# Seven tiny row loads on ScalarE's transfer queue in the second to last pair of heads, and another order of VectorE's last stage, in a decode step of gated attention with its gradients

## The chip, the core and the metric

The kernel runs on one core of one Trainium2 chip. The time is device microseconds of one execution; lower is better. A core has TensorE (PE), VectorE (DVE), ScalarE (ACT), GpSimd (POOL) and SyncE (SP), each with its own queue of instructions that it takes in order, and 16 transfer (DMA) engines that move data between HBM and the on-chip memory. SP, ACT and POOL start transfers.

## The reference

One token (D = 640) goes through attention over a cache of 4096 keys and values in 32 heads of 128, beside a small dense block with a mish activation (1728 wide); a gate g mixes the two. The kernel computes the output and the gradients of nine of the ten inputs:

```
q = (x @ wq) per head;  s = q . K * 128**-0.5;  p = softmax(s)
a = (p @ V, all heads) @ wo
h = x @ w1 + b1;  b = (h * tanh(softplus(h))) @ w2
g = sigmoid(sum(x * gate_w));  out = g * a + (1 - g) * b
gradients of sum(out * grad_out) for x, K, V, wq, wo, w1, b1, w2, gate_w
```

K and V are 33.6 MB each in bfloat16, and dK and dV as large, so nearly all of the 164 MB moved are the cache read once and its gradient written once. Since a head has one query, dV is the outer product of p and the gradient of the head's output, and dK that of the score's gradient and q.

## The kernel before

The heads are worked in 16 pairs (i = 0 to 15), four pairs to a group g. K and V of a pair are one tile each of 128 partitions x 64 keys x 128 (2 MB); seven such buffers are reused in turn. A buffer's K or V is overwritten in place by dK or dV, stored, and loaded anew by `pump` when its store has landed.

A pair is 16 slots (`slot`, from L743). In slots 0 to 7 PE transposes V in eighths into PSUM, ACT copies each to a `tch` tile (L377), and two slots later PE multiplies it with the output's gradient (L384, dP); in slots 8 to 15 the same is done with the next pair's K (S). The softmax of the pair runs in slots 2 to 8, the sums over V and K (o, dq, L433) in slots 7, 8, 13 and 14. DVE makes dV in four quarters of 128 x 2048 in slots 9, 10, 12 and 13 and dK in slot 15 and slots 0, 1 and 3 of the pair after (`outer`, L465, 1.2 us each). PSUM holds three transposed eighths. Other work is hung into slots by `plan` and `at`: `side` has a list of functions for each (pair, slot), which run in order at the slot's end. DVE sums wq against dq (`dx_sum`, L486), ACT then scales it into dwq in place (`dwq_row`, L352), and dwq is stored in column pieces: the first half by ACT in slot 8 of pair 12, the rest by POOL. The schedule is by hand: each engine's queue has its instructions in the order in which the program names them.

The last pair (i = 15) runs slots 0 to 7 and then a tail written out by hand: `last_dv(t)` and `last_dk(t)` make quarter t and, after quarters 1 and 3, start a store of half the tile on SP (L875, L881). Between them stand the o row, the last a columns, eight dwo rows on ACT with two stores of dwo on ACT (L358), five dx sums on DVE and five dwq rows on ACT. Last come the gate's gradient (L918 to L935), five transposes of the final rows (L939), their copy by DVE (L941) and three small stores on POOL (L944).

A transfer signals its landing on a semaphore. In the built program the transfers that SP and ACT start take eight semaphores in turn (numbers 0 to 7 below), nearly in the order in which the program names them, whichever of the two starts them; POOL's take eight of their own. A start is preceded by a wait for the last user of its semaphore, unless the engine has waited for that before. Around the change, in that order:

```
semaphore  start                          
0          SP   load V of pair 13
1          SP   load K of pair 14
2          SP   load V of pair 14
3          ACT  store dwq, columns of groups 0 and 1 (2560 KB)
4          SP   load K of pair 15
5          SP   load V of pair 15
6          SP   store dK of pair 12
7          SP   store dV of pair 13
0          SP   store dK of pair 13
1          SP   store dV of pair 14
```

Of the kernel before, what the change touches and what calls it, by code (L numbers as in the profile page):

```python
# [12 lines left out]
BF16 = mybir.dt.bfloat16  # L13
# [4 lines left out]
def kernel(  # L18
# [33 lines left out]
    nc = tc.nc  # L52
# [49 lines left out]
    def C(shape, dt, name):  # L102
        return const.tile(shape, dt, name=name, tag=name)
# [116 lines left out]
    def misc(shape, dt, name):  # L220
        return one_ps.tile(shape, dt, name=name, tag="misc")

    def chain(shape, dt, name):
        return one_ps.tile(shape, dt, name=name, tag="chain")
# [99 lines left out]
    def o_rows(g):  # L324
        ps = misc([P, 16, 8], F32, "o8_ps")
        nc.tensor.matmul(ps[:].rearrange("p a b -> p (a b)"), lhsT=od16[:].rearrange("p a b -> p (a b)"), rhs=idb[:],
                         start=True, stop=True)
        o8m = two.tile([P, 16, 8], F32, name="o8m", tag="o8m", bufs=1)
        nc.vector.tensor_tensor(o8m[:], ps[:], m16[:].unsqueeze(2).to_broadcast([P, 16, 8]), ALU.mult)
        nc.vector.reduce_sum(o8f[:], o8m[:].rearrange("p a b -> p b a"), axis=AX.X)  # L330
        nc.vector.tensor_copy(o8[:], o8f[:])

    def a_cols(g, c0=0, c1=RC):
        if c0 == 0:
            mst["a"] = misc([P, RC + W], F32, "a_ps")
        ps = mst["a"][:, 0:RC]
        wv = wob[g % 2][:].rearrange("p k (n c) -> p k c n", c=RC)
        for c in range(c0, c1):
            for k in range(8):
                nc.tensor.matmul(mst["a"][:, c:c + W], lhsT=wv[:, k, c, :], rhs=o8[:, k:k + 1].to_broadcast([P, W]),  # L340
                                 start=(k == 0), stop=(k == 7))
        if c1 == RC:
            if g == 0:
                nc.vector.tensor_copy(a_acc[:], ps)
            else:
                nc.vector.tensor_tensor(a_acc[:], a_acc[:], ps, ALU.add)

    def scaled(eng, dst, src, col):
        if eng is nc.vector:
            nc.vector.tensor_scalar(dst, src, col, None, ALU.mult)  # L350
        else:
            nc.scalar.mul(dst, src, col)  # L352
# [4 lines left out]
    def st_dwo(g, eng, k0=0, k1=8):  # L357
        eng.dma_start(dwo_v[g][:, k0:k1], wob[g % 2][:, k0:k1])  # L358
# [103 lines left out]
    def outer(b, col, row, q):  # L462
        n = J // 4
        j0 = q * n
        nc.vector.tensor_tensor(  # L465
            kview(b)[:, j0:j0 + n, :].rearrange("p j (a b) -> p j a b", b=2),
            col[:, j0:j0 + n, :].unsqueeze(2).to_broadcast([P, n, Dh // 2, 2]),
            row.rearrange("p (a b) -> p a b", b=2).unsqueeze(1).to_broadcast([P, n, Dh // 2, 2]),
            ALU.mult)
# [5 lines left out]
    def dq_row(i):  # L475
        dqb = two.tile([P, 2], BF16, name="dqb", tag="dqb")
        nc.vector.tensor_copy(dqb[:], st[i]["dq"][:, 0:2])  # L477
        ps = chain([P, 2, P], BF16, "dqr_ps")
        for hh in range(2):
            nc.tensor.transpose(ps[:, hh, :], dqb[:, hh:hh + 1].to_broadcast([P, P]), idb[:])  # L480
        c = 256 * (i % 4)
        nc.scalar.copy(dqrow[(i // 4) % 2][:, c:c + 256].rearrange("p (a b) -> p a b", a=2), ps[:])
# [6 lines left out]
    def dwq_row(g, c0, c1, rc, eng=nc.scalar):  # L489
        scaled(eng, wqa[:, rc, g * GC + c0:g * GC + c1], dqrow[g % 2][:, c0:c1], xf[:, rc:rc + 1])  # L490

    def st_dwq(c0, c1, eng):
        eng.dma_start(dwq_v[:, :, c0:c1], wqa[:, :, c0:c1])
# [126 lines left out]
    def at(i, s, f, *a):  # L620
        side.setdefault((i, s), []).append(lambda: f(*a))

    def plan(i, table):
        for s, tasks in table.items():
            for t in tasks:
                at(i, s, *t)
# [76 lines left out]
    plan(12, {8: [(st_dwq, 0, HC, nc.scalar)]})  # L703
    plan(14, {6: [(st_dwq, HC, HC + GC, nc.gpsimd)]})

    CA, CB = GC // 2, 3 * GC // 4
    g, i = NG - 1, NP - 2
    for k, s in enumerate((5, 6, 7, 14, 15)):
# [162 lines left out]
    def last_dv(t):  # L871
        outer(vbuf[i], st[i]["p"], Dr[g % 2][:, q, :], t)
        if t % 2:
            h = slice((t - 1) * KVW // 4, (t + 1) * KVW // 4)
            nc.sync.dma_start(dVv[i][:, h], bufs[vbuf[i]][:, h])  # L875

    def last_dk(t):
        outer(fb, st[i]["ds"], Qr[g % 2][:, q, :], t)
        if t % 2:
            h = slice((t - 1) * KVW // 4, (t + 1) * KVW // 4)  # L880
            nc.sync.dma_start(dKv[i][:, h], bufs[fb][:, h])  # L881
# [12 lines left out]
    last_dv(0)  # L894
    for rc in range(RC):
        dwq_row(g, CA, CB, rc)
    o_rows(g)
    dq_row(i)
    last_dv(1)
    a_cols(g)  # L900
    for k in range(8):
        dwo_row(g, k)
        if k % 4 == 3:
            st_dwo(g, nc.scalar, k - 3, k + 1)
    last_dv(2)
    last_dv(3)
    last_dk(0)
    last_dk(1)
    for rc in range(RC):
        dx_sum(g, NG + g, CB, GC, rc)  # L910
        dwq_row(g, CB, GC, rc)
    st_dwq(g * GC + CA, (g + 1) * GC, nc.gpsimd)
    last_dk(2)
    last_dk(3)

    fin = C([P, 3, RC], BF16, "fin")
    ga = C([P, RC], F32, "ga")
# [8 lines left out]
                                   accum_out=dgp[:])  # L926
    dg_ps = chain([P, 1], F32, "dg_ps")
    nc.tensor.matmul(dg_ps[:], lhsT=ones_f[:], rhs=dgp[:], start=True, stop=True)
    dz = C([P, 1], F32, "dz")
    nc.vector.tensor_scalar(dz[:], dg_ps[:], g_all[:], omg[:], ALU.mult, ALU.mult)  # L930
    nc.vector.tensor_scalar(fin[:, 2, :], xf[:], dz[:], None, ALU.mult)
# [5 lines left out]
    fr_ps = misc([3, RC, P], BF16, "fr_ps")  # L937
    for c in range(RC):
        nc.tensor.transpose(fr_ps[:, c, :], fin[:, :, c], idb[:])  # L939
    frow = C([3, P, RC], BF16, "frow")  # L940
    nc.vector.tensor_copy(frow[:].rearrange("r p c -> r c p"), fr_ps[:])  # L941
    for r, v in enumerate((out_0.rearrange("a b n -> (a b) n"), out_1.rearrange("a b n -> (a b) n"),
# [31 lines left out]
```

## Time and profile before

| | |
|---|---|
| median of 2 runs | 406.71 us (406.62 to 406.8) |
| the profiled execution | 405.83 us |
| its span, first to last instruction | 404.0 us |
| busy: PE, DVE, ACT, POOL | 297.2, 285.6, 246.8, 25.2 us |
| moved | 164.88 MB, mean 408 GB/s |
| mean granted clock of PE | 0.901 |

Times below count from the start of the span. In the profile's lists a line has the start, the length, the engine, the source line and operation, what is written and read, and the count; in brackets is the idle time before it and what ended it. "SPq" and "ACTq" are starts of transfers. A line of a stretch has its bounds and length, the busy time of PE, PE's weight loads, DVE, ACT and POOL with their counts, PE's granted clock, the share of time that the 16 transfer engines were busy, and GB/s.

### The profile page before, as it was taken

Reading aid. Unit: us, or ns where it says so; the run is one execution under the profiler, and the core shown is the slowest. Engines: PE = TensorE matmul, PEld = TensorE weight load, DVE = VectorE, ACT = ScalarE, POOL = GpSimd, SP = SyncE. Lnnn points to the kernel's source line nnn. Section 1 sums busy time; section 2 is a strip of 40 time slices with the busy share of each in tenths; the row PEclk is TensorE's granted clock in tenths of the full one; section 3 lists DMA queues with packets and bytes.
Section 4 is the critical chain, followed back from the end, with each engine's and each line's share of the span. In section 5 each row is a group of like instructions: output and inputs, shape, how many; then the busy total and the mean of one; then the engine's idle time right before and its main releaser. Section 6 shows DMA issues by size and latency. Waiting matters only on the chain.

```text
span 404.0 us, 13041 instructions
## 1 busy us (share of the span) xinstructions
PE 297.2 (74%) x5654; PEld 272.9 (68%) x5657; DVE 285.6 (71%) x618; ACT 246.8 (61%) x507; POOL 25.2 (6%) x50
## 2 busy tenths in 40 slices
PE   4878996998885888673989869732989897987110
PEld 3558986877775777673889769732789786886100
DVE  2767695699975969583797839642695988597930
ACT  3555462586668678761766567731567996876800
POOL 3000100002000101000001000000000100000020
PEclk9999997998999899986999989985899998999555
DMA  8999999999999999999999999999999999999991
GB/s 275 426 399 434 420 423 417 430 418 420 423 422 427 391 421 429 427 431 430 428 423 428 426 427 426 425 426 432 431 406 400 414 428 419 422 430 422 420 386 44
DMA packets 15963, 164.88 MB, mean 408 GB/s; under 512 B 1713, under 2 KB 1905, under 8 KB 6178
## 3 DMA queue, kind: packets, MB, share of 16 engines
q1 hardware_dynamic: 8832, 94.08, 55.7%
q0 software_dynamic: 5472, 63.42, 37.3%
q10 hardware_dynamic: 1602, 6.56, 4.1%
q8 instruction: 44, 0.72, 0.7%
q14 instruction: 13, 0.11, 0.1%
HBM read 82.03 MB, written 82.03 MB: 406 GB/s over the span
## 4 chain that ended last, share of the span: by engine, by line
DMA 34%; issue 23%; PE 20%; DVE 12%; ACT 5%; POOL 2%; SPq 1%; POOLq 0%; ACTq 0%; DVEq 0%
DMA wq<-in_A_wq_dram 10%; DMA out_dram<-kv 8%; PE tr L374 8%; DVE kv L465 7%; DMA wq<-in_B_w_dram 6%; DMA wo<-in_A_wo_dram 5%; DMA kv<-in_A_k_cache_dram 5%; ACT tch L377 2%; PE dP L384 2%; PE o L433 2%; PE S L384 2%; PE dq L433 1%; PE q_ps L277 1%; PE a_ps L340 1%; DVE wq L486 1%
## 5 line engine op out<-in xcount | busy, mean ns | idle before, releaser
L374 PE MATMUL tr<-idf,kv 128*128 128x128 f32 x1024 | 172.1, 294 | 36.0 <-DMA kv<-in_A_v_cache_dram 20.0
L377 ACT COPY tch<-tr 128x512 f32<-128x512 f32 x256 | 144.2, 587 | 83.8 <-PE tr L374 78.6
L374 PEld LDWEIGHTS tr<-idf,kv 128*128 128x128 f32 x1024 | 118.6, 150 | 41.7 <-issue 36.9
L384 PEld LDWEIGHTS <-tch 128*128 128x128 bf16 x2048 | 89.5, 99 | 27.9 <-ACT tch L377 21.8
L465 DVE TENSOR_TENSOR kv<-p_dup,Dr 128x2048 bf16<-128x2048 bf16 x64 | 76.7, 1220 | 4.4 <-ACT p_dup L424 4.1
L465 DVE TENSOR_TENSOR kv<-ds_dup,Qr 128x2048 bf16<-128x2048 bf16 x64 | 76.8, 1220 | 0.4
L433 PEld LDWEIGHTS <-kv 128*128 128x128 bf16 x2048 | 59.1, 97 | 2.7 <-issue 1.6
L384 PE MATMUL dP<-dR,tch 128*128 128x48 bf16 x1024 | 47.3, 185 | 9.3 <-ACT tch L377 9.0
L384 PE MATMUL S<-qR,tch 128*128 128x48 bf16 x1024 | 48.1, 187 | 6.9 <-ACT tch L377 5.7
L290 DVE SCALAR_TENSOR_TENSOR junk<-wo,da_bc 128x640 bf16<-128x640 bf16 x32 | 26.3, 822 | 13.5 <-DMA wo<-in_A_wo_dram 12.7
L433 PE MATMUL o<-e_m,kv 128*128 128x48 bf16 x1024 | 32.4, 186 | 0.2 <-issue 0.2
L433 PE MATMUL dq<-ds_m,kv 128*128 128x48 bf16 x1024 | 30.6, 183 | 2.1 <-DVE ds_m L455 1.9
L736 POOL DMA_DIRECT2D out_dram<-kv x25 | 13.4, 537 | 296.0 <-DVE kv L465 278.6
L352 ACT ACTIVATE wq<-dqrow,xf 128x1024 bf16<-128x1024 bf16 (+2 forms) x30 | 25.1, 860 | 1.2 <-DVE wq L486 0.8
L486 DVE SCALAR_TENSOR_TENSOR wq<-wq,dqrow 128x1024 bf16<-128x1024 bf16 (+2 forms) x30 | 25.1, 863 | 0.2
L439 DVE TENSOR_TENSOR o<-o,rz 128x2 f32<-128x2 f32 x16 | 2.5, 158 | 26.5 <-PE o L433 26.5
L398 DVE TENSOR_REDUCE m<-S 64x1 f32<-64x64 f32 x32 | 7.0, 219 | 15.8 <-PE S L384 15.6
L424 ACT ACTIVATE p_dup<-e_m,rz 64x128 bf16<-64x128 bf16 x32 | 12.7, 397 | 7.8 <-DVE rz L418 7.4
L352 ACT ACTIVATE wo<-da_bc,o8f 128x640 bf16<-128x640 bf16 x20 | 15.9, 824 | 1.5 <-PE a_ps L340 0.9
L406 DVE TENSOR_REDUCE negM<-mt 64x1 f32<-64x64 f32 x32 | 7.1, 222 | 11.5 <-PE mt L403 10.8
L480 PE MATMUL dqr_ps<-idb,dqb 128*128 128x128 bf16 x32 | 4.9, 241 | 13.7 <-DVE dqb L477 13.7
L459 ACT COPY ds_dup<-ds_m 64x128 bf16<-64x128 bf16 x32 | 9.5, 297 | 8.1 <-DVE ds_m L455 7.6
(163 smaller groups left out, 253.2 us busy)
## 6 DMA issues: line engine op xcount, KB each, us to landing
out_dram<-kv POOLq DMA_DIRECT2D x25, 2048.0 KB, 19.8
kv<-in_A_v_cache_dram SPq DMA_DIRECT2D x16, 2048.0 KB, 19.8
kv<-in_A_k_cache_dram SPq DMA_DIRECT2D x15, 2048.0 KB, 20.6
out_dram<-kv SPq DMA_DIRECT2D x5, 2048.0 KB, 26.2
wo<-in_A_wo_dram SPq DMA_DIRECT2D x4, 1280.0 KB, 20.9
out_dram<-kv SPq DMA_DIRECT2D x4, 1024.0 KB, 20.5
out_dram<-wo POOLq DMA_DIRECT2D x3, 1280.0 KB, 26.8
wq<-in_A_wq_dram SPq DMA_DIRECT2D x2, 1280.0 KB, 9.5
```

The source lines that it names most:

```text
L290: nc.vector.scalar_tensor_tensor(junk[:], in0=wob[g % 2][:, k, :], scalar=1.0, in1=da_bc[:], op0=ALU.mult, op1=ALU.mult, accum_out=do8[g % ...
L352: nc.scalar.mul(dst, src, col)
L374: nc.tensor.transpose(tp[:, t, :], src[:, 4 * c + t, :], idf[:])
L377: nc.scalar.copy(dst[:].rearrange("p a b e -> p (a b e)").bitcast(F32), tp[:].rearrange("p a b -> p (a b)"))
L384: nc.tensor.matmul(ps[:, 4 * B:4 * B + W].rearrange("p (a b) -> p a b", b=4), lhsT=src[:, t, :, e], rhs=col[:, e, :, :].rearrange("p a b - ...
L406: nc.vector.tensor_reduce(negM[HS[hh]], mt[HS[hh], 64 * hh:64 * hh + 64], axis=AX.X, op=ALU.max, negate=True)
L424: nc.scalar.activation(p[HS[hh]], e_m[i % 2][HS[hh], :, hh].unsqueeze(2).to_broadcast([64, J, 2]), ACT.Copy, scale=st[i]["rz"][HS[hh], hh: ...
L433: nc.tensor.matmul(st[i][key][:].rearrange("p (a b) -> p a b", b=2), lhsT=src[:, j, :], rhs=rhs[:, j, :].unsqueeze(1).to_broadcast([P, W / ...
L459: nc.scalar.copy(ds[HS[hh]], ds_m[i % 2][HS[hh], :, hh].unsqueeze(2).to_broadcast([64, J, 2]))
L465: nc.vector.tensor_tensor(kview(b)[:, j0:j0 + n, :].rearrange("p j (a b) -> p j a b", b=2), col[:, j0:j0 + n, :].unsqueeze(2).to_broadcast ...
L486: nc.vector.scalar_tensor_tensor(w, in0=w, scalar=1.0, in1=dqrow[g % 2][:, c0:c1], op0=ALU.mult, op1=ALU.mult, accum_out=dq_acc[:, rc, par ...
L736: eng.dma_start(dst, bufs[b][:, 0:J * Dh])
```

## The change

Seven loads of n rows of 32 bytes each (n = 4, 8, 9, 10, 11, 12, 13) from wq into tiles that nothing reads are started by ACT in slot 2 of pair 14. With them seven of the eight semaphores change hands: in the order above they stand behind the store of dV of pair 13, take semaphores 0 to 3, then SP's store of dK of pair 13 takes 4, and the last three loads take 5 to 7. In DVE's tail the second quarter of dV comes before the o row, the third before the a columns, one quarter of dK before and one after the dx sums and dwq rows, and the last two go between the parts of the final rows.

```diff
+    MARK = (4, 8, 9, 10, 11, 12, 13)
+    marks = [C([16, 16], BF16, f"mark{n}") for n in MARK]
+
+    def mark():
+        for n, t in zip(MARK, marks):
+            nc.scalar.dma_start(t[0:n], A_wq[0:n, 0:16])
+
+    plan(14, {2: [(mark,)]})
...
     last_dv(0)
     for rc in range(RC):
         dwq_row(g, CA, CB, rc)
+    last_dv(1)
     o_rows(g)
     dq_row(i)
-    last_dv(1)
+    last_dv(2)
     a_cols(g)
...
-    last_dv(2)
     last_dv(3)
     last_dk(0)
-    last_dk(1)
     for rc in range(RC):
         dx_sum(g, NG + g, CB, GC, rc)
         dwq_row(g, CB, GC, rc)
     st_dwq(g * GC + CA, (g + 1) * GC, nc.gpsimd)
-    last_dk(2)
-    last_dk(3)
+    last_dk(1)
...
     nc.tensor.matmul(dg_ps[:], lhsT=ones_f[:], rhs=dgp[:], start=True, stop=True)
+    last_dk(2)
     dz = C([P, 1], F32, "dz")
...
         nc.tensor.transpose(fr_ps[:, c, :], fin[:, :, c], idb[:])
+    last_dk(3)
     frow = C([3, P, RC], BF16, "frow")
```

## The prediction

> **What bounds the kernel now.** I read the page's slices first, then stretches of the tail, then the landings of single transfers, then ACT's timeline where the change goes in, and the chain of waits last.
>
> ```profile
> DMA  8999999999999999999999999999999999999991
> 384.00:388.00 4.00, 1.25 (x7) 0.91 (x7) 2.33 (x10) 0.00 (x0) 0.76 (x1) 0.50 1.02 426
> ...
> 396.00:398.00 2.00, 0.00 (x0) 0.00 (x0) 0.00 (x0) 0.00 (x0) 0.00 (x0) 0.50 0.07 29
> 398.00:400.00 2.00, 0.00 (x0) 0.00 (x0) 0.00 (x0) 0.00 (x0) 0.00 (x0) 0.50 0.06 25
> 400.00:402.00 2.00, 0.00 (x0) 0.00 (x0) 0.00 (x0) 0.00 (x0) 0.00 (x0) 0.50 0.07 29
> ```
>
> The transfers bound it: their engines are full from the second slice to about 392 us, at some 0.42 MB per us. From 396 to 402 their share is 0.06 to 0.07, one engine of sixteen: one engine ran behind the others and alone sets the end. That leaves slack in front of the end: the last big store is issued at 383.72 and lands 18.9 us later, at 402.6.
>
> ```profile
> 383.72 0.33 SPq L881 DMA_DIRECT2D out_dram<-kv  x1
> ...
> out_dram<-kv SPq DMA_DIRECT2D x1, 1024.0 KB, 18.9
> ```
>
> The next lines are what the new loads meet: issue on the left, and in the other view the us to landing.
>
> ```profile
> 312.43 0.62 ACTq L493 DMA_DIRECT2D out_dram<-wq  x1
> out_dram<-wq ACTq DMA_DIRECT2D x1, 2560.0 KB, 48.8
> 340.40 1.38 SPq L736 DMA_DIRECT2D out_dram<-kv  x1
> out_dram<-kv SPq DMA_DIRECT2D x1, 2048.0 KB, 25.3
> 341.89 0.89 SPq L736 DMA_DIRECT2D out_dram<-kv  x1
> out_dram<-kv SPq DMA_DIRECT2D x1, 2048.0 KB, 30.7
> 344.90 0.59 ACT L377 COPY tch<-tr 128x512 f32<-128x512 f32 x1 [0.57 <-PE tr L374]
> 345.58 1.26 ACT L377 COPY tch<-tr 128x512 f32<-128x512 f32 x2
> ```
>
> So the store of dwq's first half (ACT) lands at 361.2, dK of pair 12 at 365.7 and dV of pair 13 at 341.89 + 30.7 = 372.6. The reader is to see that ACT reaches the place of the new loads, after its copy of slot 2, at 345.5.
>
> ```profile
> 350.52 0.63 PE tr L374 x4
> ...
> 375.06 4.63 DVE kv L465 x4
> 379.69 1.73 DVE wq L486 x10
> 381.41 2.27 DVE kv L465 x2
> ...
> 389.27 1.05 POOL out_dram L944 x2
> ```
>
> From 350.52 to the end the chain is computing alone (PE, ACT, DVE): no transfer is waited for. Work held up here moves one for one.
>
> **The change, part by part.**
>
> *The seven loads.* A transfer started by SP or ACT signals on one of eight semaphores, taken in turn, and its start waits until the semaphore's last user has landed. In the changed program's order the seven starts wait for: V of pair 13, K of pair 14 and V of pair 14 (all landed by 341.2, since PE works on that V then), dwq's first half (361.2), V of pair 15 (before 358.57, when PE transposes it), dK of pair 12 (365.7) and dV of pair 13 (372.6). All seven stand in ACT's queue between the copies of slots 2 and 3 of pair 14. So ACT stands from 345.5 until dV of pair 13 has landed.
>
> When is that? Until then everything already issued runs as before. One store is gone from in front of it: the quarter of dwq that POOL issues at 361.36 needs ACT's scalings behind the loads. It has 655 KB, 41 KB for each engine, at 0.42/16 = 0.026 MB per us 1.6 us. I take 371.0; bounds 372.6 (it took nothing on the lagging engine) and 364.5 (no engine lags: by the trace's semaphore updates fifteen of the sixteen parts of this store were in by 366.1, less 1.6).
>
> The start itself: ACT's start at 381.16 held the next scaling until 381.54, 0.4 us; the six before the last lie inside the stall. Their traffic, 67 rows of 32 bytes for which nothing computes, goes to engines that are running empty: 0, and were they full, no more than any of the 1.2 KB stores at the end. ACT goes on at 371.4 with the copy that began at 345.58: delay 25.8 us.
>
> No row shows ACT standing for a landing, so I weigh this by the nearest: SP stands 287.6 us in all before its loads for landings, and POOL 59.1 us before L493 for ACT. The Trainium skill says in "DMA: Bandwidth & Descriptors" (Anatomy of one DMA) that transfer engines wait on no semaphore and that every such wait is served on the issuing sequencer before dispatch. By that rule ACT's copies stand behind the load and the sum is as here; without it, the first rival.
>
> Behind ACT stand PE (three transpose buffers, so it stops three slots on), DVE (all of pair 14 past its dx sums), SP's dV of pair 14 and POOL's dwq stores. Corrections: PE wakes at half clock; the stretch 341.18 to 344.59 was granted 0.50 and so did 1.7 us of work in 3.4, a cost of 0 (ACT was the busier, 6.67 of 7 us after 345) to 1.7, I take 1.0. PE's wait of 0.8 us for K of pair 15 at 350.52 goes. Delay 25.8 + 1.0 - 0.8 = 26.0 us.
>
> *SP's waits.* Its lanes shift too: dK of pair 13, issued at 345.75, now waits for K of pair 15 (350.4, by the same semaphore rule). It is 4.6 us later in a full queue behind 6 MB, cost 0; without that cover, 4.6. The later starts wait for the tiny loads, then long landed: 0.
>
> *DVE's tail.* In the old time scale: dV quarters 0 and 1 at 370.3 to 372.6, so dV's first half is issued at 372.8 (was 374.19). The reduction of o waits no more on PE but starts at 372.65 (was 372.05), 0.6 later, and with it ACT's dwo rows, its last dwq rows and POOL's last dwq store (384.6, was 383.94). Quarter 2, a_acc, quarter 3 end at 376.9 (dV's second half; was 377.45), dK 0, five dx sums and dK 1 at 380.9 (was 379.72). dK 2 now fills the 0.74 us wait for dg_ps and dK 3 the 0.79 us wait for the final transposes; dK's second half comes at 385.3 (was 383.72), the final rows' copy ends at 387.1 instead of 389.0, its three stores are issued from 387.4 to 388.4. DVE's gain is 1.9 us, behind the lagging engine's 402.6 worth nothing as things stand; with the stall the chain of computing sets the end and it counts.
>
> *The end.* Old scale plus 26.0. From dV's second half on, 1.05 + 0.66 + 1.05 + 0.66 + 0.66 + 1.05 = 5.1 MB are issued from 377 to 385.3: at 0.42 they take 12.2 us and, begun 1 us after the issue, never run dry: 390.2, and with 1.3 us of spread between engines 391.5. The lagging engine has caught up by then, having only dK of pair 13 (131 KB, 5 us) left after 371. The last small store, issued by 388.4, lands between 3 us later (the fastest parts of the first one before, 389.27 to 392.2) and 6.5 (as the page of issues has it, behind a backlog): I take 4, 392.4. The Trainium skill's "DMA: Bandwidth & Descriptors" (Anatomy of one DMA) fits a fixed 2.0 us to a small transfer; by that it would be hidden and the time 0.9 lower. Landing to the end of the span was 404.0 - 402.6 = 1.4. Span: 392.4 + 1.4 + 26.0 = 419.8 us, +15.8 on 404.0. The profiled execution took 405.83, 1.83 over its span: 421.6. It stood 0.9 under the median of 406.71, so the medians' scale gives 421.6 to 422.5; I say 422.0.
>
> **The rivals.**
>
> *Not slower: ACT's copies don't stand behind the loads.* If the starts wait aside, or their landings are in when ACT comes, seven starts of 0.34 to 0.66 us remain, 2.4 to 4.6 us of ACT, and only the tail's order changes. The end would still be the lagging engine's 402.6: 405 to 407 us. It decides below a stall of 402.6 - 391.5 = 11 us, ACT going on before 356.6; 2% is reached at a stall of about 19 us, 364.5. For it: no row of before shows ACT standing for a transfer. Against it: the queue's own length. V of pair 15, dK of 12 and dV of 13 are 6.3 MB, issued in one queue from 340.02; at 0.42 alone they take 15 us, to 355, and two other queues still hold stores that land at 361.2 and 366.4.
>
> *A shorter stall.* If the lagging engine isn't behind in this run, dV of pair 13 is in at 364.5: 6.5 us less, 415.5. Against it: every landing of SP's stores from 340 on has that late part.
>
> *A longer one.* PE stays at half clock through the two pairs left, as it does after 375.31 in the profile, or the small stores take their 6.5 us and the loads land at 372.6: 426 to 430.
>
> **How the numbers follow.** My case 0.80; shorter stall 0.07, about half of it over 2%; not slower 0.08; longer 0.05. About 2% (8.1 us) is what a measurement of this kernel can tell from no change. Slower: 0.80 + 0.04 + 0.05 = 0.89. Same: 0.03 + 0.06 = 0.09. Faster: 0.02. The range runs from the shorter stall's 415.5 to the sum of the upper bounds (1.6 later landing, 0.7 more of cold PE, 2.5 for the small stores on 421.6): 426.
>
> **What would show it.** Right: an idle stretch of some 25 us on ACT before the copy of slot 3 of pair 14, ending within 1 us of the landing of dV of pair 13; PE and DVE idle in it; transfer share falling well under 0.9 from about 370 to 384; no single engine left over at the end. DVE's tail without the waits for dg_ps and fr_ps. Wrong: ACT's copies running on at 346, or a stall that ends at 361 or 366, or an end still set by one late engine.

## The result, and the profile after

The changed kernel takes 423.56 us (median of 2 runs, 423.17 and 423.95) against 406.71: 1.0414 times as long, 95% interval 1.037 to 1.0459. The forecast was 422.0, in a range of 415.5 to 426.0. The profiled execution is the one of 423.95, with a span of 422.2. It ran 1.9 us late already ahead of the change (V of pair 15 starts loading at 341.90, before at 340.02).

First the slices of transfer share and of PE's clock, from the page, then the stretches from the change to the end:

```profile
PEclk9999996998996999777999889759999996559955
DMA  8999999999999999999999999999999999904786
352.00:362.00 10.00, 0.00 (x0) 0.00 (x0) 0.00 (x0) 0.00 (x0) 0.00 (x0) 0.50 1.03 437
362.00:372.00 10.00, 0.00 (x0) 0.00 (x0) 0.00 (x0) 0.00 (x0) 0.00 (x0) 0.50 0.66 281
372.00:384.00 12.00, 11.06 (x204) 10.82 (x204) 4.88 (x12) 9.47 (x21) 0.00 (x0) 0.71 0.03 10
384.00:400.00 16.00, 12.72 (x312) 11.94 (x307) 13.74 (x35) 11.72 (x28) 0.84 (x1) 1.00 0.76 306
400.00:408.00 8.00, 1.88 (x42) 1.77 (x42) 7.06 (x20) 5.16 (x9) 0.00 (x0) 0.68 0.65 268
408.00:412.00 4.00, 1.06 (x7) 0.91 (x7) 3.83 (x14) 3.47 (x7) 0.00 (x0) 0.50 1.01 414
412.00:416.00 4.00, 0.19 (x2) 0.00 (x0) 2.39 (x2) 0.00 (x0) 2.14 (x4) 0.50 1.01 406
416.00:418.00 2.00, 0.00 (x0) 0.00 (x0) 0.00 (x0) 0.00 (x0) 0.22 (x1) 0.50 1.00 346
418.00:420.00 2.00, 0.00 (x0) 0.00 (x0) 0.00 (x0) 0.00 (x0) 0.00 (x0) 0.50 0.10 25
```

The reader is to see three things. For 20 us, 352 to 372, no engine computes at all. While that lasts the transfers run out of work: full until 362, two thirds busy until 372, and 0.03 for the next 12 us, in which the computing has started again but has nothing ready to store. And from 408 on they are full to within a microsecond and a half of the last landing (419.6): where before had one engine of sixteen at work for six microseconds, all of them now finish together.

ACT's timeline around the new loads, and the longest waits from 344 to 375 (total, times, longest):

```profile
344.59 1.26 ACT L377 COPY tch<-tr 128x512 f32<-128x512 f32 x2
345.29 26.91 ACTq L711 DMA_DIRECT2D mark<-in_A_wq_dram  x7
372.30 1.07 ACT L377 COPY tch<-tr 128x512 f32<-128x512 f32 x2 [26.45 <-DMA out_dram<-kv]
```

```profile
ACT tch L377 <- DMA out_dram<-kv: 26.4, 1, 26.4
PEld L384 <- ACT tch L377: 25.9, 1, 25.9
PE dP L384 <- ACT tch L377: 25.6, 1, 25.6
```

The seven starts span 26.91 us of ACT's queue, and the copy after them names the store they waited for: `out_dram<-kv`, a pair's gradient. The single starts tell which one. Three go out at 345.29, 345.61 and 345.96; the fourth at 362.62, when dwq's first half lands; the fifth at 362.95; the sixth at 366.62, as dK of pair 12 lands; the seventh at 371.89, as dV of pair 13 lands, 28.3 us after its issue. PE then waits for ACT's copy, 25.6 us (its weight loads 25.9), and everything behind PE with it.

The end, from the timeline:

```profile
408.56 4.37 SPq L889 DMA_DIRECT2D out_dram<-kv  x2
411.35 1.22 DVE L465 TENSOR_TENSOR kv<-ds_dup,Qr 128x2048 bf16<-128x2048 bf16 x1
412.22 0.82 POOL L493 DMA_DIRECT2D out_dram<-wq  x1 [22.41 <-ACT wq L352]
412.49 1.91 DVE L949 COPY frow<-fr_ps 3x640 bf16<-3x640 bf16 x1
414.68 1.53 POOL L952 DMA_DIRECT2D out_dram<-frow  x3 [1.65 <-DVE frow L949]
```

DVE's waits for dg_ps and fr_ps are gone: the last quarter of dK runs up to 412.5 and the copy of the final rows follows. The last big store (dwq's, POOL, 412.22) lands at 419.0, the last small one at 419.6, and the span ends 2.6 us later.

### The profile page after: what moved, and what is told of

It reads as the page before. It is cut to its first block, busy times and chain, and to the rows that moved or that the text cites. A ratio compares the mean times of both kernels' runs of the same rounds, so it can differ in the third digit from the quotient of the medians.

```text
span 422.2 us, 13051 instructions
## 1 busy us (share of the span) xinstructions
PE 298.1 (71%) x5654; PEld 274.9 (65%) x5657; DVE 285.4 (68%) x618; ACT 246.2 (58%) x507; POOL 25.1 (6%) x50
## 4 chain that ended last, share of the span: by engine, by line
issue 43%; DMA 26%; PE 12%; DVE 9%; ACT 3%; POOL 2%; SPq 1%; DVEq 0%; POOLq 0%; ACTq 0%
DMA out_dram<-kv 11%; DMA wq<-in_A_wq_dram 9%; DVE kv L465 6%; DMA wq<-in_B_w_dram 6%; PE tr L374 4%; PE o L433 2%; POOL out_dram L744 2%; PE dP L384 1%; ACT tch L377 1%; PE S L384 1%; PE b_ps L574 1%; PE a_ps L340 1%; DVE wq L486 1%; PE q_ps L277 1%; DVE wq L350 1%
## 5 line engine op out<-in xcount | busy, mean ns | idle before, releaser
L433 PEld LDWEIGHTS <-kv 128*128 128x128 bf16 x2048 | 60.4, 98 | 4.2 <-issue 3.2
L418 DVE RECIPROCAL rz<-z 128x2 f32<-128x2 f32 x16 | 2.7, 170 | 31.0 <-PE z L416 30.8
## 6 DMA issues: line engine op xcount, KB each, us to landing
kv<-in_A_k_cache_dram SPq DMA_DIRECT2D x15, 2048.0 KB, 20.5
```

What stands on the lines that cost most here:

```text
L433: nc.tensor.matmul(st[i][key][:].rearrange("p (a b) -> p a b", b=2), lhsT=src[:, j, :], rhs=rhs[:, j, :].unsqueeze(1).to_broadcast([P, W / ...
```

## The experiments

In these runs the kernel before had a median of 406.3. "Lost" is the median less 406.3; "stall" is ACT's idle time before the copy of slot 3 of pair 14.

| run | what differs | median us | ratio, 95% interval | stall | lost |
|---|---|---|---|---|---|
| tail_only | new tail, no loads | 406.31 | 0.9995 (0.9982 to 1.0008) | none | 0 |
| loads_only | loads, old tail | 423.56 | 1.042 (1.0396 to 1.0444) | 25.4 | 17.3 |
| loads_on_sp | SP starts the loads | 408.62 | 1.0057 (1.0039 to 1.0075) | 0 | 2.3 |
| three_loads | 4, 8, 9 rows | 407.3 | 1.0024 (1.0008 to 1.0039) | 0.5 | 1.0 |
| four_loads | 4 to 10 rows | 411.08 | 1.0123 (1.0092 to 1.0154) | 14.3 | 4.8 |
| six_loads | 4 to 12 rows | 417.5 | 1.0269 (1.0232 to 1.0306) | 22.7 | 11.2 |
| sixteen_rows | seven of 16 rows | 422.76 | 1.0407 (1.0383 to 1.043) | 25.3 | 16.5 |
| loads_last | loads after all else | 407.0 | 1.0013 (0.9996 to 1.003) | 0 | 0.7 |
| split_7_engines | no loads, a store cut | 417.64 | 1.0278 (1.0256 to 1.0301) | none | 11.3 |
| split_16_engines | no loads, cut otherwise | 410.74 | 1.0116 (1.0094 to 1.0138) | none | 4.4 |

### Each half of the change alone

tail_only takes the loads out again; loads_only keeps them and puts DVE's tail back.

```diff
# tail_only, against the changed kernel
...
-    plan(14, {2: [(mark,)]})
# loads_only, against the changed kernel
-    last_dv(1)
     o_rows(g)
     dq_row(i)
-    last_dv(2)
+    last_dv(1)
     a_cols(g)
...
+    last_dv(2)
     last_dv(3)
     last_dk(0)
+    last_dk(1)
...
-    last_dk(1)
+    last_dk(2)
+    last_dk(3)
...
-    last_dk(2)
...
-    last_dk(3)
```

> VectorE's new tail without the seven loads. Theory (ACT stands behind its own transfer starts, and before the change one late transfer engine ends the kernel at 402.6): the tail's gain of about 1.9 us on VectorE stays hidden, 405.5 to 407.5 us, and the last landing is still the late engine's. Rival (the new order itself costs, by stores issued later at the end): 409 or more.

> The seven loads with the old tail. Theory: the stall on ACT is the same 26 to 27 us, and now VectorE's slower tail counts in full: 1.7 to 2 us over the changed kernel's 423.6, 424.5 to 426. Rival (part of the loss is the new tail's): under 421.

The tail alone changes nothing. Its final rows are stored 2.7 us sooner than before (0.5 of it because this execution was ahead by that much already at V of pair 15), and one transfer engine still sets the end. From the timeline and the page of issues of tail_only, then its stretches:

```profile
386.60 1.53 POOL L944 DMA_DIRECT2D out_dram<-frow  x3 [1.67 <-DVE frow L941]
```

```profile
out_dram<-kv SPq DMA_DIRECT2D x1, 1024.0 KB, 17.7
```

```profile
396.00:398.00 2.00, 0.00 (x0) 0.00 (x0) 0.00 (x0) 0.00 (x0) 0.00 (x0) 0.50 0.06 25
398.00:400.00 2.00, 0.00 (x0) 0.00 (x0) 0.00 (x0) 0.00 (x0) 0.00 (x0) 0.50 0.07 29
400.00:402.00 2.00, 0.00 (x0) 0.00 (x0) 0.00 (x0) 0.00 (x0) 0.00 (x0) 0.50 0.05 20
```

The last half of dK is issued at 384.52 and lands 17.7 us later, at 402.2; fifteen of its sixteen parts were in by 396.6.

The loads alone cost all of it, 423.56, and that misses the 424.5 to 426 on record: the new tail was to be worth 1.9 us behind the stall, and nothing of it shows in the medians. With 2 and 4 runs these alone leave a microsecond or two open; the traces tell more. In loads_only ACT goes on at 370.98; its last part, from the timeline, the stretches and the page of issues:

```profile
410.32 0.82 POOL L493 DMA_DIRECT2D out_dram<-wq  x1 [21.79 <-ACT wq L352]
415.62 1.53 POOL L952 DMA_DIRECT2D out_dram<-frow  x3 [4.47 <-DVE frow L949]
```

```profile
408.00:412.00 4.00, 0.56 (x2) 0.50 (x2) 3.15 (x11) 2.03 (x5) 0.82 (x1) 0.50 1.01 412
412.00:416.00 4.00, 0.69 (x5) 0.41 (x5) 2.48 (x5) 0.00 (x0) 0.38 (x1) 0.50 1.01 394
416.00:418.00 2.00, 0.00 (x0) 0.00 (x0) 0.00 (x0) 0.00 (x0) 1.15 (x3) 0.50 0.71 233
```

```profile
out_dram<-frow POOLq DMA_DIRECT2D x3, 1.2 KB, 2.2
```

The transfers are full from 408 to 416 here too. From dV's second half on, the same 5.1 MB have to drain, 12.2 us at 0.42 MB per us, and that half is issued 32.8 us after ACT goes on (403.79) against 32.3 in the changed kernel (404.56 after 372.30). So the big stores end at nearly the same distance behind the stall (at 419.0, 46.7 us after ACT goes on, against 417.9, 46.9 after, in loads_only), whatever DVE does in between. The old tail's final rows come later (415.62 to 417.15) but find the queues running empty and land in 2.2 us, the last at 418.5, 47.5 after ACT goes on. The new tail's come sooner, stand behind the stores still draining, and land in 4.2 us, the last at 419.6, 47.3 after. That is 0.2 us gained.

### Who stands, and for how many semaphores

loads_on_sp changes the issuing queue, four_loads, three_loads and six_loads the number, sixteen_rows the shape.

```diff
-            nc.scalar.dma_start(t[0:n], A_wq[0:n, 0:16])
+            nc.sync.dma_start(t[0:n], A_wq[0:n, 0:16])     # loads_on_sp
...
-    MARK = (4, 8, 9, 10, 11, 12, 13)
+    MARK = (4, 8, 9)                    # three_loads
+    MARK = (4, 8, 9, 10)                # four_loads
+    MARK = (4, 8, 9, 10, 11, 12)        # six_loads
+    MARK = (16,) * 7                    # sixteen_rows
```

> The same seven loads at the same place with the new tail, but started by SP, so that SP's queue stands for the landings and ACT's does not. The starts wait for the same kind of landings (the last for dK of pair 12, then the store of dK of pair 13 for dV of pair 13). Theory: ACT, PE and VectorE run on; SP's three next stores are issued at about 371 instead of 346 to 364, the other transfer engines run dry for some 5 us, the late one hardly: 406 to 410 us. Rival (the loads' own transfers or the waiting itself cost, wherever they are started): 420 to 425.

> The first three loads only (4, 8 and 9 rows) on ACT, new tail. They wait for loads that have landed when ACT comes to them (the last, V of pair 14, is what PE works on then). Theory: no stall on ACT, 1 us of starts, hidden: 405.5 to 408 us, and ACT's copies go on at once. The store of dK of pair 13 now waits for dwq's first half (361), in SP's queue only: no cost over 1 us. Rival (each load costs its share): 413 to 414.

> The first four loads only (4, 8, 9 and 10 rows) on ACT, new tail. The last of the four waits for the store of dwq's first half (361 to 363), not for dV of pair 13 (372). Theory: a stall of 16 us, 10.7 less than with seven, all of it computing on the path: 411 to 414 us. Rival (each load costs its share of the 16.9 us lost): 416 to 417.

> The first six loads (4 to 12 rows) on ACT, new tail; the last waits for the store of dK of pair 12 (365 to 367), 6 us before the seventh's landing. From no stall with three loads, 14.3 us of stall with four (411.1) and 26.5 with seven (423.6), about 9.7 us of a stall are hidden and the rest counts one for one. Theory: a stall of about 20.5 us, 10.8 us over 406.3: 416 to 418.5. Rival (a share for each load): 421.

> Seven loads of 16 rows each in place of 4 to 13 rows, same place, same waits, new tail. Theory: the number of rows and which transfer engines they fall on is nothing to the time: 422 to 425 us, the stall ending at the landing of dV of pair 13. Rival (loads of an uneven number of rows are slow to finish or hold single engines): 415 or less.

On SP the same seven starts wait too, and the kernel loses 2.3 us instead of 17. The last of them waits for dK of pair 12 (366.2), and the store of dK of pair 13, next in SP's queue, for dV of pair 13 (373.2). The longest waits of loads_on_sp from 340 to 376, on SP (the second is that of V of pair 15's load, ahead of the change), SP's starts from 362, ACT's timeline at 345.65, and two stretches:

```profile
SPq L711 <- DMA out_dram<-wq: 18.9, 1, 18.9
SPq L131 <- DMA out_dram<-kv: 11.3, 1, 11.3
SPq L744 <- DMA out_dram<-kv: 5.6, 1, 5.6
```

```profile
364.31 3.24 SPq L711 DMA_DIRECT2D mark<-in_A_wq_dram  x4
373.26 2.52 SPq L744 DMA_DIRECT2D out_dram<-kv  x3
```

```profile
345.65 0.33 ACT L411 ACTIVATE e_m<-S,negM 64x64 bf16<-64x64 f32 x1 [0.53 <-DVE negM L406]
```

```profile
362.00:372.00 10.00, 8.25 (x193) 7.76 (x192) 7.77 (x26) 7.19 (x19) 0.84 (x1) 1.00 0.45 169
376.00:384.00 8.00, 1.40 (x24) 1.24 (x21) 7.10 (x23) 6.53 (x10) 0.00 (x0) 0.58 1.01 426
```

Behind SP stand only stores, and ACT computes on. The transfers do run short, 0.45 busy from 362 to 372, but the stores that were held up fill them again from 376 on. What they lost comes out of the slack in front of the late engine: the last store lands at 405.3, and its other fifteen parts are in at 404.6 to 404.8, where before they were in by 396.6. The wait is in the queue that issues, and its price is what else stands in that queue.

With fewer loads the stall ends at an earlier landing, as the order of semaphores has it. The copy behind the loads in four_loads, six_loads and sixteen_rows:

```profile
360.91 1.07 ACT L377 COPY tch<-tr 128x512 f32<-128x512 f32 x2 [14.30 <-DMA out_dram<-wq]
```

```profile
367.37 1.07 ACT L377 COPY tch<-tr 128x512 f32<-128x512 f32 x2 [22.74 <-DMA mark<-in_A_wq_dram]
```

```profile
372.19 1.07 ACT L377 COPY tch<-tr 128x512 f32<-128x512 f32 x2 [25.31 <-DMA out_dram<-kv]
```

Four loads end with dwq's first half (`out_dram<-wq`). Six hold ACT for 22.7 us (20.5 were expected) against 26.4 with all seven, which wait for dV of pair 13 besides. (The second line names a mark, the last transfer before it. dwq's first half had landed at 364.9; dK of pair 12 landed at 365.8, while ACT's fifth start still ran, until 366.3, so that its wait held ACT no longer.) Three loads hold ACT for 0.5 us, because their semaphores' users had landed; then it is SP's store of dK of pair 13 that waits, until 364.98, and that costs at most 1.0. The rows make no difference that shows: with 16 each, the stall is 1.1 us shorter than the changed kernel's (and as long as that of loads_only), the time 0.8 us.

Stall against loss, from the table: 0.5 costs 1.0, 14.3 costs 4.8, 22.7 costs 11.2, 25.3 to 26.4 costs 16.5 to 17.3. Between 14.3 and 25.4 the loss grows by 12.5 for 11.1 us. A stall counts from where ACT came to the loads, and that differs between executions (the first load starts at 343.80 in six_loads, at 346.32 in sixteen_rows), so the steps in between are uneven; the time at which ACT goes on is the better measure. From there to the end of the span it is 48.0 us in four_loads, 48.9 in six_loads and 49.9 to 50.5 with seven loads. Before the change it was 58.4, from the same copy at 345.58. So 8 to 10 us are hidden behind the late engine, where the forecast put 11.

### Only the starts, without what they hold up

loads_last calls the seven loads as ACT's last work, after the final rows.

```diff
-    plan(14, {2: [(mark,)]})
...
         nc.gpsimd.dma_start(v, frow[r:r + 1].rearrange("r p c -> r (p c)"))
+    mark()
```

> The same seven loads on ACT as its very last work, behind the last scalings and stores, with the new tail. ACT stands for the last big stores' landings, but nothing stands behind it. Theory: the wait costs nothing but the last load's own landing after the last store: 406 to 409 us. Rival (seven such loads on ACT cost by themselves, wherever they are): 415 or more.

407.0: the loads themselves, their 67 rows and their completions, cost 0.7 us here (from 0.2 gained to 1.2 lost by the interval). All the rest comes from where they stand.

### An attempt to relieve the late engine

With the loads out, the late engine is what the kernel ends on. The landings of the marks in three_loads (4 rows all in by 349.7; of 8 rows seven parts by 351.5 and one at 366.6) say that it is not among the engines that 4 rows use but among those that 8 rows use, and two kernels cut the store of dK of pair 13 so that some engines carry less of it.

```diff
-        eng.dma_start(dst, bufs[b][:, 0:J * Dh])
+        r = 0
+        for n in (49, 49, 30) if dct is kbuf and i == 13 else (P,):   # split_16_engines: (48, 48, 32)
+            eng.dma_start(dst[r:r + n], bufs[b][r:r + n, 0:J * Dh])
+            r += n
```

> No loads, new tail; the store of dK of pair 13 is cut into three starts of 49, 49 and 30 rows. By the landings of the loads of 4, 8 and 9 rows in the changed kernel the late engine is among the fifth to eighth. If 49 rows run on seven engines, that engine gets 2 rows of 16 KB instead of 8: 98 KB less, 3.7 us. Theory (this one engine alone sets the end without the loads): the last landing comes 3 to 4 us earlier, 402 to 404 us. Rival (the end is set by the sum of all traffic or by computing): 406 to 407, or more by the seven engines' longer share.

> Control for the split: the same store cut into 48, 48 and 32 rows, all of which divide by 16, so that each engine has its 8 rows as before. Theory: as the new tail alone, 405.5 to 407 us. Rival (three starts in place of one help or cost by themselves): as the other split, or over 407.5.

Both miss. In split_7_engines one engine alone runs on until 415.6; its stretch, and dV of pair 14 on the page of issues, of split_7_engines and then of tail_only:

```profile
408.00:412.00 4.00, 0.00 (x0) 0.00 (x0) 0.00 (x0) 0.00 (x0) 0.00 (x0) 0.50 0.06 27
```

```profile
out_dram<-kv SPq DMA_DIRECT2D x1, 2048.0 KB, 39.4
```

```profile
out_dram<-kv SPq DMA_DIRECT2D x1, 2048.0 KB, 25.6
```

The first 49 rows landed in seven parts, six at 365.7 to 370.4 and the seventh at 382.6: the late engine is one of the seven that got 14 rows in the first two pieces alone, where the whole store gives each of sixteen 8, so the cut loaded it where it was to relieve it. The Trainium skill, "DMA: Bandwidth & Descriptors" (Why a DMA increments its semaphore by 16 and not by 1), says that a transfer issued by SP or ACT runs on the largest number of engines up to 16 that divides its rows, and on the lowest-numbered ones; by that rule the late one is the fifth to the seventh engine, since four rows miss it and 49 rows, on seven, meet it. The seven parts of 49 rows agree with the rule; which engine it is by number, no row says.

The control shows that cutting alone costs 4.4 us: with 48, 48 and 32 rows the late engine ends at 407.4 instead of 402.2. Why, stays open; that rows go to other engines than in the whole store is a guess that wasn't tried. No kernel of this study beats the one before.

## Why the prediction was right

- **ACT stands behind the loads until dV of pair 13 has landed: right.** The wait names the store and the copy follows its landing by 0.4 us. loads_on_sp shows that it is the queue that matters, the shorter lists that it is the semaphores' last users. The rule of the Trainium skill that the prediction cited, waits served on the issuing sequencer ("DMA: Bandwidth & Descriptors", Anatomy of one DMA), agrees with the 26.4 us of ACT here.
- **The landing, 371.0: measured 371.9** in an execution that was 1.9 us late; from its issue 28.3 us against a forecast of 29.1 (371.0 less 341.89).
- **The cold PE: mis-sized.** Forecast +1.0, less the 0.8 of K of pair 15, net 0.2. Measured: the delay is 26.7 at ACT's copy (372.30 against 345.58) and 27.6 at the division of o (379.79 against 352.18), net 0.9. PE's clock stayed at half until 378.98, 6.0 us after PE's first product (372.94), where the row used for the estimate had 3.4. In four_loads and six_loads it stayed so for 3.4 and 3.2 us, and there the way from ACT's copy to that division took 6.4 us, 0.2 less than before, in place of 7.5. So the size of this term differs from run to run by about 1.1 us.
- **A later store on SP costs nothing: right**, as far as three_loads shows it: there the store of dK of pair 13 waits until 364.98, longer than forecast here, and the whole loss is 1.0.
- **DVE's tail: the step that failed** is "with the stall the chain of computing sets the end and it counts". The waits went as forecast and the final rows' stores left at 414.68, against 387.4 plus 27.6, 415.0. But behind the stall the 5.1 MB of stores set the end, and they start with dV's second half, which the new tail brings only 0.5 us sooner (32.3 us after ACT goes on, 32.8 in loads_only); loads_only is the same 423.56 without it. The working had the drain at 391.5 and the small stores at 392.4 in the old scale, so it took a difference of 0.9 for the bound to be computing. Where queues are still draining, an earlier small store only waits longer.
- **The drain: right.** 391.5 plus 27.6 is 419.1; the last big store landed at 419.0, the last small one at 419.6, 3.9 us after its issue, where 4 was taken. The 1.3 us of spread between engines in that working comes from no row that it shows; the parts of the last big store landed within 0.6 us (418.45 to 419.04).
- **The end of the span: mis-sized.** 1.4 us were taken from landing to end, 2.6 measured.

The sum: 0.9 from the later landing, 0.7 from the cold PE, 1.2 at the end of the span, less 0.4 for the last landing (392.4 forecast, 419.6 less 27.6 is 392.0) make the 2.4 by which the span of 422.2 stands over the 419.8 forecast. From span to median 2.2 were added and 1.4 measured, which leaves the 1.6 by which 423.56 stands over 422.0. That the failed step did no harm to the number is luck: the two bounds lay 0.9 us apart in the working, so either gave nearly the same end. Of the rivals, "not slower" holds with the loads on SP, at ACT's end or only three of them; the break-even that it named, 11 us, is measured at 8 to 10.

## What to carry to other kernels

A transfer's start may wait for the landing of an unrelated transfer that used the same semaphore eight starts earlier, so a start on an engine that also computes can hold its whole work: before adding one, count back eight in issue order and see when that user lands. Put starts whose semaphore is not free on a queue with no computing behind it: the same seven loads cost 17 us on ACT and 2.3 on SP. Slack in front of a late transfer engine is worth what it measures (here 8 to 10 us), and an earlier issue helps only if it starts what then drains.

## What the runs showed that I had not expected

- Cutting one 2 MB store in three made the late engine end 5.2 us later (407.4 against 402.2) even with rows that sixteen divides, for the same bytes.
- After 20 us without a matmul PE was granted half its clock for the first 6.0 us of nearly full work. The Trainium skill, "TensorE: Matmul & The Clock Gate" (Part 1: The HAM clock gate), gives about 3.4 us of sustained work to warm up; four_loads (3.4) and six_loads (3.2) agree, while the changed kernel, loads_only (6.2) and sixteen_rows (5.6) took nearly twice that. In the changed kernel the clock changes at 351.67, 378.98 and 402.87, which are 8 and 7 times 3.413 us apart, and in every other run here too the changes lie a whole multiple of 3.413 us apart. That the wait depends on where between two such marks the work begins fits these five runs; no run was made to try it.
- The Trainium skill, "DMA: Bandwidth & Descriptors" (Anatomy of one DMA), fits a fixed 2.0 us to a small transfer. The final rows take 2.2 us in loads_only, where the queues are running empty (0.71 busy from 416 to 418), and 4.2 us in the changed kernel, behind draining stores.
- The span ended 2.6 to 3.0 us after the last landing where POOL's small store was the last (the changed kernel, loads_only, four_loads), and 0.9 to 1.4 where SP's big store was (before, tail_only, loads_on_sp).
